# One written list for the chunk loop of a recurrence that feeds a mixture of experts: preparation five chunks ahead, two strided transposes, filler products spread

## The chip, the cores and the metric

The kernel runs on one core of a Trainium2 chip. The core's engines work beside each other and meet through semaphores: TensorE (PE in the profile, its weight loads are PEld) multiplies and transposes into PSUM, VectorE (DVE) and ScalarE (ACT) work on whole tiles, GpSimd (POOL) masks and scatters, and SyncE (SP) issues most of the DMA transfers. Each engine takes its instructions strictly in the order in which they are written for it. The metric is device time in microseconds (us); smaller is better.

## What is computed

The program is a linear recurrence over 768 positions for 4 x 8 heads of width 40, and then a layer of eight experts, of which each row uses the best one. Cut to what matters:

```python
for t in range(S):                                   # attention, S = 768
    y[:, :, t] = einsum('bhd,bhde->bhe', r_t, state)
    Sa = einsum('bhde,bhe->bhd', state, a_t)
    state = state * w_t - outer(Sa, b_t) + outer(v_t, k_t)
...
logits = x @ w_gate                                  # x is y, 3072 rows of 320
expert_idx = argmax(logits)
for e in range(8):
    out[mask_e] = gate_w[mask_e] * (relu(x[mask_e] @ w1[e]) @ w2[e])
```

All data are 32-bit floats.

## The kernel before

**Tiling.** The recurrence is cut into NC = 24 chunks of C = 32 positions. Inside a chunk it is written in closed form with a 32 x 32 triangular matrix per head, which has to be inverted; between chunks only the state is handed on. All 32 heads go together, as 16 pairs or 8 groups.

**The stages of a chunk.** Each is a Python generator whose parts (between its yields) can be placed one by one in the written order. One letter names each:

- p, preparation of a chunk (`step_prep`): a first part with two scans over the decays w (L231, L233) and a small reciprocal, which then issues the DMA loads of the next chunk's w; a second part with two products (`kbmul` L240, `qmul` L245) that scale k, b, r and a, and then further loads. In the start list its pieces have letters of their own: W and a (loads), s (scan), j and q (the two products).
- E (`step_e`): 16 products of a chunk's scaled rows on TensorE (L254), copies into M2c on ScalarE (`m2`, L262), copies into Q (`m1`, L275), and a triangular mask on POOL (`m1_mask`, L280).
- t (`tops`): the inversion for four chunks at once. Its first part transposes M2c into Tt on VectorE (L285), copies to ML on ScalarE and clears parts of Tt on POOL; 14 steps of two VectorE operations each follow (L297, L299); its last part transposes Tt into Tc2 (L302) and Tc (L303).
- B (`merge`): finishes one chunk's inverse: products (L314), copies to Q1, named NB (L318), products (L323), copy into Tc (L325).
- The recurrence itself: R (L347, then ScalarE's copy RS<-psS, L350), U (L357, copies L362), S (L371, then VectorE's product into SVR, L376), and SVR is what the next chunk's R reads.
- The output side: T, K and u are transposes on TensorE with copies on ScalarE, A (L409, VectorE's mask L412) and y (L426, L437) give the chunk's result, and r routes two chunks' rows to their experts and sends them out to the DRAM buffer Xs.
- i writes a seventh of Xs with initial values (648 KB each).

Products on TensorE that go to ps_g share four rotating PSUM blocks of one bank each.

**What sets the order.** Nothing is scheduled by the compiler in this part. A start list (START) is written out by hand: it prepares chunks 0 to 12 and, with an @ ahead of a letter, already places most of the parts of chunks 0 to 3. From chunk I0 = 4 a loop places the parts by a fixed pattern of letters (ORDER, one for even and one for odd chunks), in which a number stands for a share of the inversion of the next four chunks (SPLIT). Preparation runs nine chunks ahead (`s = i + 9` in `step_prep`), E eight ahead. KB and Q have NKB = 9 buffers each, so the load of chunk s + 1's KB has to wait until chunk s - 8 has been transposed; it is therefore the last part of p. The w tile (Wt) and the a tile (AT) have one buffer each. START also holds 72 products of a constant tile scn (L668, 128 x 512, bf16) whose results nobody reads. After the loop a short list (TAIL) ends chunk 23, and the expert stage follows with its own order.

Of the kernel before, what the change touches and what calls it, by code (L numbers as in the profile page):

```python
# [13 lines left out]
U8 = mybir.dt.uint8  # L14
# [5 lines left out]
B, H, S, D = 4, 8, 768, 40  # L20
# [4 lines left out]
E = 8  # L25
# [9 lines left out]

ORDER = (".1 R T A p R T A U U E 2.3 B p E B S E y u u K S B 1 B y K r p",
         ".1 R T A p R T A U U E r 2.3 B p E r B S E y u u K S B 1 B y K r p")
SPLIT = (0, 0.3, 0.5, 0.7, 1)  # L40
TAIL = "R A T U b E S y u K r"

START = ("W0 a0 W1 a1 w22 s0 j0 q0 c5 W2 a2 s1 j1 q1 w9 W3 a3 e0 w3 n0 s2 j2 q2 e1 w3 n1 c7 z0 W4 a4 s3 j3 q3 e2 w3 "
# [8 lines left out]
ENGS = {mybir.EngineType.PE, mybir.EngineType.Activation, mybir.EngineType.DVE, mybir.EngineType.Pool,  # L54
        mybir.EngineType.SP}
AALT = 3
I0 = 4

YW = tuple(int(c == NC - 1) for c in range(NC))
AW = tuple(4 * (c == NC - 1) for c in range(NC))  # L60
# [64 lines left out]
def attention(tc, nc, d, ctx, Xs, okt, sent):  # L125
# [53 lines left out]
    at = lambda ring, c: ring[c % len(ring)]  # L179

    flat = lambda t: t.rearrange("p a b->p (a b)")
    early = lambda s: (0, 1, 2, 0, 2, 0, 2)[s] if s < 7 else 0

    def buf(s):
        v = lambda t: t[:, 0:528].rearrange("p (a b)->p a b", b=33)
# [51 lines left out]
    def kbmul(s, eng):  # L237
        f = buf(s)[1]
        kb = at(KB, s).rearrange("p a (k i)->p a k i", k=2)
        eng.tensor_tensor(kb, kb, f[:, :, 0:32].unsqueeze(2).broadcast_to([128, 16, 2, 32]), ALU.mult)  # L240
        G_.tensor_copy(F0[:, s, :], f[:, :, 32])

    def qmul(s, eng):
        g = gview(s).unsqueeze(2).broadcast_to([128, 16, 2, 32])
        eng.tensor_tensor(at(Q, s), buf(s)[2].rearrange("p t a i->p a t i"), g, ALU.mult)  # L245
# [11 lines left out]
    def m2(s, e):  # L257
        m2, n0 = M2c[0], (s % 4) * 8
        for j in range(2):
            for ty in range(2):  # L260
                bb = 32 * (j * 2 + ty)
                A.copy(m2[bb:bb + 32, :, n0:n0 + 8].rearrange("p t n->p n t"), e[j][32:64, :, ty])  # L262

    def m1v(s, e):
        q = at(Q, s)
# [16 lines left out]

    def tops(k):
        def first():
            V.transpose(flat(Tt), flat(M2c[0]))  # L285
            A.copy(at(ML, k)[:, 0:32], M2c[0][:, 0:16, :].rearrange("p t n->p n t"))
            G_.memset(Tt[:, 0:16, 16:32], 0.0)
            for h in (16, 8, 4, 2, 1):
                G_.memset(bass.AP(Tt.tensor, Tt[:, h, 0:1].offset, [Tt.ap[0], [66 * h, 16 // h], [32, h], [1, h]]), 0.0)
            G_.memset(flat(Tt)[:, 0:1024:33], -1.0)  # L290

        def step(j):
            n = 15 - j
            t = tmp[:, :2 * j * n].rearrange("p (h a b)->p h a b", a=j, b=n)
            bcast = lambda a0, b0, sa, sb: bass.AP(Tt.tensor, Tt[:, a0, b0:b0 + 1].offset,
                                                   [Tt.ap[0], [528, 2], [sa, j], [sb, n]])
            V.tensor_tensor(t, bcast(0, j, 32, 0), bcast(j, j + 1, 0, 1), ALU.mult)  # L297
            u = bcast(0, j + 1, 32, 1)
            V.tensor_tensor(u, u, t, ALU.subtract)  # L299

        def last():
            V.transpose(flat(Tc2), Tt.rearrange("p a b->p b a")[:, 16:32])  # L302
            V.transpose(flat(at(Tc, k)), flat(Tt))  # L303

        return [(2, first)] + [(2 * (0.12 + 2 * j * (15 - j) / 960), lambda j=j: step(j)) for j in range(14, 0, -1)] + [
            (3.1, last)]

    def merge(c):
        t, m, n0 = at(Tc, c // 4), flat(at(ML, c // 4)), c % 4 * 8
        quads = [slice(bb, bb + 32) for bb in range(0, 128, 32)]  # L310
        q = g4([128, 8, 16])
        for x in range(8):
            for b in quads:
                TE.matmul(q[b, x], m[b, (n0 + x) * 16:(n0 + x) * 16 + 32], Tc2[b, :, n0 + x],  # L314
                          start=True, stop=True, tile_position=(b.start, b.start))
        yield
        for b in quads:
            A.copy(Q1[b, :, b.start % 64 + 16:b.start % 64 + 32], q[b])  # L318
        yield
        z = g4([128, 8, 16])  # L320
        for x in range(8):
            for b in (slice(0, 64), slice(64, 128)):
                TE.matmul(z[b, x], Q1[b, x], t[b, 0:16, n0 + x], start=True, stop=True, tile_position=(b.start, b.start))  # L323
        yield
        A.copy(t[:, 0:16, n0:n0 + 8].rearrange("p a n->p n a"), z)  # L325

    def kbt(c):
        kb, ks = at(KB, c), at(KS2, c)
# [23 lines left out]
    def ustage(c):  # L352
        sv, t, rs = at(SVS, c), at(Tc, c // 4), held["rs"]
        u = psU[:, 0:320].rearrange("p (h e)->p h e", e=40)
        for h in range(8):
            for bb in range(0, 128, 32):
                TE.matmul(u[bb:bb + 32, h], t[bb:bb + 32, :, c % 4 * 8 + h], rs[bb:bb + 32, h, bb // 32 % 2 * 40:bb // 32 % 2 * 40 + 40],  # L357
                          start=True, stop=True, tile_position=(bb, bb))
        yield
        for bb in range(4):  # L360
            j, ty = divmod(bb, 2)
            A.copy(sv[32:64, j * 8:j * 8 + 8, TO[ty]:TO[ty] + 40], u[32 * bb:32 * bb + 32])  # L362
# [195 lines left out]
        if i < NC:  # L558
            yield from ustage(i)

    def step_e(i):
        s = i + 8
        if s < NC:
            e = estage(s)
            yield
            m2(s, e)
            yield
            m1(s, e)
            m1_mask(s)
# [20 lines left out]
        if 0 <= i - 1 < NC:  # L590
            yield from route_a(i - 1, held["x"])

    def step_prep(i):
        s = i + 9
        if s < NC:
            scan(s)
            if s + 1 < NC:
                load_w(s + 1, kb=False)
            yield
            kbmul(s, V)  # L600
            qmul(s, V)
            if s + 1 < NC:
                load_a(s + 1)
                yield
                load_kb(s + 1)

    def step_merge(i):
        if i < NC:
# [9 lines left out]
             "S": step_s, "y": step_y, "u": step_ut, "K": step_kbt, "r": step_route, "p": step_prep,  # L618
             "B": step_merge}
    es = {}  # L620
    with tc.manual_schedule(engines=ENGS):
        to = tops(0)
        gens = {}
        for op in START.split():
# [46 lines left out]
            elif op[0] == "c":  # L671
# [18 lines left out]
                if n == 7:  # L690
# [4 lines left out]
    manual = tc.manual_schedule(engines=ENGS)
    manual.__enter__()
    for i in range(I0, NC):
        tl = []
        if 4 * (i // 4 + 1) < NC:
            o, at_ = tops(i // 4 + 1), 0.0  # L700
            tot = sum(w_ for w_, _ in o)
            for w_, f in o:
                if SPLIT[i % 4] - 1e-9 <= at_ / tot < SPLIT[i % 4 + 1] - 1e-9:
                    tl.append((w_, f))
                at_ += w_

        def invert(n):
            while tl and n > 0:
                w_, f = tl.pop(0)
                f()  # L710
                n -= w_

        if True:
            for step in ORDER[i % 2].split():
                if step in steps:
                    k = step + str(i - (step == "r" and i % 2) + (step == "B"))
                    if k not in gens:
                        gens[k] = steps[step](int(k[1:]))
                    next(gens[k], None)
                else:  # L720
                    invert(float(step))
            invert(99)
            for k in list(gens):
                if k != f"r{i}":
                    for _ in gens.pop(k):
                        pass
# [321 lines left out]
```

## Time and profile before

| | |
|---|---|
| time, median of 3 runs | 695.79 us (692.59 to 697.78) |
| the profiled execution | 697.46 us, of which its span 695.7 us |
| mean granted TensorE clock over the span | 0.869 |
| TensorE busy, the recurrence up to 456.7 us | 390.8 us |
| moved by DMA | 93.59 MB, 135 GB/s on average |

The span is the time from the first to the last instruction. [...] In the rows of the profile a line such as L350 is a line of the kernel above, `out<-in` names the tiles without buffer numbers, and idle time stands with the engine and operation that ended it.

### The profile page before, as it was taken

The numbers are of one execution on the slowest core, as the hardware profiler recorded it, in microseconds if no ns is written. First come the engines' busy times: TensorE is split into PE (matmuls) and PEld (weight loads), VectorE is DVE, ScalarE is ACT, GpSimd is POOL, SyncE is SP. The second block draws the span as 40 slices with busy tenths as digits, with TensorE's granted clock in tenths as the row PEclk, the third lists the DMA queues.
The fourth block names the chain that finished last, engine by engine and source line by source line (L and its number), as shares of the span: only waits on it lengthen the run. The fifth ranks groups of instructions, "written<-read, shape, count | busy, mean of one in ns | idle before, by whom it ended". The sixth has DMA issues, their size and how long they took to land.

```text
span 695.7 us, 27306 instructions
## 1 busy us (share of the span) xinstructions
PE 618.5 (89%) x11867; PEld 560.5 (81%) x11867; DVE 446.3 (64%) x876; ACT 399.7 (57%) x915; POOL 125.5 (18%) x239
## 2 busy tenths in 40 slices
PE   7477888579999989799999999989999999999994
PEld 3246778568888879798889888769999999999994
DVE  8895457898768585767554323368567577585641
ACT  2635777677677777778855765455436345255220
POOL 1331212232212121212301101110110211201111
PEclk9676788569787787889996989969999999999997
DMA  7887345524444343443332323488473564552101
GB/s 213 195 219 211 108 130 169 148 88 114 131 113 134 107 127 108 126 112 99 102 100 85 88 92 95 133 257 258 127 233 110 170 224 129 169 185 81 57 0 33
DMA packets 47318, 93.59 MB, mean 135 GB/s; under 512 B 10553, under 2 KB 27066, under 8 KB 47128
## 3 DMA queue, kind: packets, MB, share of 16 engines
q1 hardware_dynamic: 44632, 83.85, 41.1%
q0 software_dynamic: 2560, 7.92, 3.2%
q8 instruction: 96, 1.57, 1.0%
q14 instruction: 30, 0.25, 0.1%
HBM read 79.19 MB, written 13.21 MB: 133 GB/s over the span
## 4 chain that ended last, share of the span: by engine, by line
PE 62%; ACT 12%; issue 10%; DMA 7%; DVE 7%; SPq 1%; POOL 0%; POOLq 0%; DVEq 0%; ACTq 0%
PE ps_g L323 4%; PE psS L347 4%; PE psS L371 4%; PE ps_g L409 4%; PE psY L426 4%; DMA out<-yo,tok 3%; PE m_yp L857 3%; PE m_yp L858 3%; PE m_yp L859 3%; PE m_hp L839 3%; PE m_hp L838 3%; PE ps_g L254 3%; PE m_hp L840 3%; PE ps_g L393 3%; PE psU L357 3%
## 5 line engine op out<-in xcount | busy, mean ns | idle before, releaser
L412 DVE TENSOR_TENSOR Y<-ps_g,mask 64x512 f32<-64x512 f32 x48 | 32.8, 684 | 78.6 <-PE ps_g L409 78.1
L262 ACT COPY M2c<-ps_g 32x256 f32<-32x256 f32 x96 | 57.7, 601 | 31.2 <-PE ps_g L254 29.7
L871 POOL DMA_INDIRECT out<-yo,tok x32 | 30.6, 958 | 200.3 <-DVE yo L870 136.9
L857 PE MATMUL m_yp<-w2h,hx 128*128 128x320 f32 x192 | 60.9, 317 | 0.0
L858 PE MATMUL m_yp<-w2l,hx 128*128 128x320 f32 x192 | 59.2, 308 | 0.0
L859 PE MATMUL m_yp<-w2h,hx 128*128 128x320 f32 x192 | 59.1, 308 | 0.0
L846 DVE SCALAR_TENSOR_TENSOR hx<-m_hp,hx 128x384 fp32r<-128x384 f32 (+1 forms) x128 | 42.7, 386 | 24.3 <-ACT hx L844 24.0
L844 ACT ACTIVATE hx<-m_hp 128x448 fp32r<-128x448 f32 x64 | 34.9, 545 | 40.3 <-PE m_hp L842 40.3
L376 DVE TENSOR_TENSOR SVR<-psS,F 40x640 f32<-40x640 f32 x46 | 37.8, 822 | 29.8 <-PE psS L371 29.2
L371 PE MATMUL psS<-SVS,KS 128*40 128x40 f32 x1472 | 43.1, 220 | 13.1 <-ACT SVS L362 5.7
L280 POOL TENSOR_SCALAR_AFFINE_SELECT Q<-Q 32x512 f32<-32x512 f32 x48 | 37.5, 781 | 90.5 <-ACT Q L275 81.3
L371 PEld LDWEIGHTS psS<-SVS,KS 128*40 128x40 f32 x1472 | 37.4, 133 | 18.8 <-ACT SVS L362 9.3
L362 ACT COPY SVS<-psU 32x320 f32<-32x320 f32 x96 | 40.0, 417 | 18.5 <-PE psU L357 16.7
L338 ACT COPY KS<-ps_g 64x416 f32<-64x416 f32 x96 | 49.0, 510 | 1.2
L254 PE MATMUL ps_g<-Q,KB 128*64 128x64 f32 x768 | 36.5, 267 | 14.1 <-DVE Q L245 7.1
L347 PE MATMUL psS<-SVR,Q 128*64 128x80 f32 x768 | 44.3, 288 | 4.2 <-DMA SVR<-in_VR 4.2
L838 PE MATMUL m_hp<-x,w1h 128*128 128x448 f32 x128 | 47.4, 370 | 0.4 <-ACT x L822 0.4
L839 PE MATMUL m_hp<-x,w1h 128*128 128x448 f32 x128 | 47.6, 372 | 0.0
L254 PEld LDWEIGHTS ps_g<-Q,KB 128*64 128x64 f32 x768 | 33.0, 178 | 17.9 <-DVE Q L245 8.9
L840 PE MATMUL m_hp<-x,w1l 128*128 128x448 f32 x128 | 47.3, 369 | 0.0
L426 PE MATMUL psY<-Y,KS 128*40 128x32 f32 x1504 | 38.9, 212 | 9.1 <-issue 9.1
L347 PEld LDWEIGHTS psS<-SVR,Q 128*64 128x64 f32 x768 | 39.7, 181 | 8.1 <-POOL Q L280 4.5
(165 smaller groups left out, 1491.8 us busy)
## 6 DMA issues: line engine op xcount, KB each, us to landing
w2r<-in_w SPq DMA_DIRECT2D x8, 1280.0 KB
w1r<-in_w SPq DMA_DIRECT2D x8, 1024.0 KB
VU<-in_VT SPq DMA_DIRECT2D x48, 160.0 KB
SVR<-in_VR SPq DMA_DIRECT2D x48, 104.0 KB
SVS<-in_VS SPq DMA_DIRECT2D x24, 208.0 KB
KB<-in_KB SPq DMA_DIRECT2D x30, 160.0 KB
KB<-in_KBP SPq DMA_DIRECT2D x9, 512.0 KB
Xs<-xr SPq DMA_DIRECT2D x7, 648.0 KB
```

Source lines behind the costliest of these rows:

```text
L254: TE.matmul(e[j][:, x], kb[:, p, :], q[:, p], start=True, stop=True, tile_position=(0, 64 * j))
L262: A.copy(m2[bb:bb + 32, :, n0:n0 + 8].rearrange("p t n->p n t"), e[j][32:64, :, ty])
L338: A.copy(ks[0:64, u * 8 + z:u * 8 + 8:2], ts[u][64 * z:64 * z + 64])
L347: TE.matmul(psS[64 * j:64 * j + 64, h, 0:80], q[:, p].rearrange("e t i->e (t i)"), sr[:, :, h, j * 64:j * 64 + 40], start=True, stop=True, ...
L371: TE.matmul(psS[TR[ty], h, j * 40:j * 40 + 40], ks[:, p, o:o + 40], sv[:, p, o:o + 40], start=True, stop=True, tile_position=(0, o))
L426: TE.matmul(py[TR[ty], p], ks[:, p, o:o + 40], y2[:, ty, p, :], start=True, stop=True, tile_position=(0, o))
L838: TE.matmul(hp, w1h[:, k, s], xh[:, k], start=k == 0, stop=False)
L839: TE.matmul(hp, w1h[:, k, s], xl[:, k], start=False, stop=False)
L840: TE.matmul(hp, w1l[:, k, s], xh[:, k], start=False, stop=False)
L857: TE.matmul(yp, hh[:, ft, qs], w2h[:, ft], start=ft == 0, stop=False)
L858: TE.matmul(yp, hh[:, ft, qs], w2l[:, ft], start=False, stop=False)
L859: TE.matmul(yp, hl[:, ft, qs], w2h[:, ft], start=False, stop=ft == 7)
```

## The change

START ends after chunk 3's first E part, the first inversion and R of chunk 0. Everything after it, up to chunk 23, is one list, ORDER, of 751 entries: a letter with its chunk number places the next part of that stage, t the next part of the running inversion, and f two filler products. There are 48 f in it. Preparation now takes the chunk's number from the list, and the list places it five chunks ahead of the recurrence at first (p5 in chunk 0) and up to eight ahead in the middle (p17 in chunk 9); the KB load is issued together with the w load. M2c and Tc are stored with the head index outside, so that the copies and products which touch one head read or write rows without gaps, while the transposes L285 and L303 (L299 and L317 after) read or write with a step. Chunk 1's first Q copies carry the mask with them on VectorE (`m1v`, which was there but unused, L283). Stage A of chunks 0 to 2 uses the form of the later chunks (AALT).

The filler goes to one of the four ps_g blocks; START's went to psY.

```diff
-ORDER = (".1 R T A p R T A U U E 2.3 B p E B S E y u u K S B 1 B y K r p",
+ORDER = ("y0 M2 j4 B0 K0 B0 q4 A0 i0 B0 B0 B1 p5 B1 p5 K0 f U0 E5 p6 U0 S0 S0 E4 u0 p6 i1 E5 E5 f B1 E4 p7 u0 B1 p7 R1  "
...
-AALT = 3
-I0 = 4
+AALT = 0
...
-                A.copy(m2[bb:bb + 32, :, n0:n0 + 8].rearrange("p t n->p n t"), e[j][32:64, :, ty])
+                A.copy(m2[bb:bb + 32, n0:n0 + 8, :], e[j][32:64, :, ty])
...
-            V.transpose(flat(Tt), flat(M2c[0]))
-            A.copy(at(ML, k)[:, 0:32], M2c[0][:, 0:16, :].rearrange("p t n->p n t"))
+            V.transpose(flat(Tt), M2c[0].rearrange("p n t->p t n"))
+            A.copy(at(ML, k)[:, 0:32], M2c[0][:, :, 0:16])
...
-            V.transpose(flat(at(Tc, k)), flat(Tt))
+            V.transpose(at(Tc, k).rearrange("p n a->p a n"), flat(Tt))
...
-    def step_prep(i):
-        s = i + 9
+    def step_prep(s):
         if s < NC:
             scan(s)
             if s + 1 < NC:
-                load_w(s + 1, kb=False)
+                load_w(s + 1)
             yield
             kbmul(s, V)
             qmul(s, V)
             if s + 1 < NC:
                 load_a(s + 1)
-                yield
-                load_kb(s + 1)
...
+        if op == "f":
+            hot = g4([128, 512])
+            for _ in range(2):
+                TE.matmul(hot, scn[:, 0:128], scn[:, 0:512], start=True, stop=True)
+            continue
```

How the order moves is seen at three places. The first is VectorE around the first inversion. KB_87 and Q_88 are chunk 4's tiles, Q_82 is chunk 1's. Before:

```order
L233 SCALAR_TENSOR_TENSOR G_93<-Q_78,RC 128x528
L285 STREAM_TRANSPOSE Tt<-M2c 128x1024
L240 TENSOR_TENSOR KB_87<-KB_87,KB_77 128x1024
L245 TENSOR_TENSOR Q_88<-VU,G_93 128x1024
L297 TENSOR_TENSOR tmp<-Tt 128x28
L299 TENSOR_TENSOR Tt<-Tt,tmp 128x2x14
```

Now, with the end of the inversion:

```order
L247 SCALAR_TENSOR_TENSOR G_93<-Q_78,RC 128x528
L299 STREAM_TRANSPOSE Tt<-M2c 128x1024
L283 TENSOR_TENSOR Q_82<-ps_g,mask 32x8x32 x4
L311 TENSOR_TENSOR tmp<-Tt 128x28
...
L316 STREAM_TRANSPOSE Tc_121<-Tt 128x512
L317 STREAM_TRANSPOSE Tc_115<-Tt 128x32x32
L254 TENSOR_TENSOR KB_87<-KB_87,KB_77 128x1024
L259 TENSOR_TENSOR Q_88<-VU,G_93 128x1024
```

Chunk 4's two products stand behind the inversion, and chunk 1's four masked copies have come to VectorE. The second place is the SP queue's loads after the start, around the w load of chunk 6 (KB_73). Before:

```order
L202 DMA Q_78<-in_W 40x529 x2
L195 DMA KB_73<-in_KBP 128x1024
L208 DMA VU<-in_A 40x16x32
L209 DMA VU<-in_A 40x16x32
L213 DMA SVR<-in_VR 32x832 x2
L214 DMA SVS<-in_VS 32x1664
L680 DMA VU<-in_czero 24x1024 x2
L681 DMA Y_105<-in_czero 24x1024
```

Now:

```order
L239 DMA Y_105<-in_RT 40x512
L240 DMA Y_105<-in_RT 40x512
L231 DMA VU<-in_VT 40x1024
L232 DMA VU<-in_VT 40x1024
L623 DMA Xs<-xr 128x4x324
L216 DMA Wt<-in_W 40x529 x2
L209 DMA KB_73<-in_KBP 128x1024
L222 DMA AT<-in_A 40x512
L223 DMA AT<-in_A 40x512
```

Chunk 6 is loaded behind the first blocks of the loop and one block of Xs, and no longer ahead of chunk 1's values. The third place is TensorE in the middle of the loop, from chunk 10's key transpose (KB_81) past its R (Q_82) to the next recurrence product. Before, where L254 is stage E of chunk 18:

```order
L334 MATMUL ps_g<-ident,KB_81 128x104 x8
L323 MATMUL ps_g<-Tc_115,NB 64x16 x16
L499 MATMUL ps_g<-gt,cg 128x16
L500 MATMUL ps_g<-gt,cg 128x16
L347 MATMUL psS<-SVR,Q_82 64x80 x16
L383 MATMUL ps_g<-ident,SVR 104x40 x16
L409 MATMUL ps_g<-RT,VU 64x2x32 x16
L357 MATMUL psU<-RS,Tc_115 32x40 x32
L254 MATMUL ps_g<-Q_80,KB_79 64x64 x16
```

Now, where L268 is stage E of chunk 17 and L718 the filler:

```order
L348 MATMUL ps_g<-ident,KB_81 128x104 x8
L440 MATMUL psY<-Y_105,KS_123 40x32 x32
L423 MATMUL ps_g<-RT,VU 64x2x32 x16
L268 MATMUL ps_g<-Q_78,KB_77 64x64 x16
L328 MATMUL ps_g<-Tc_121,ML_117 32x16 x32
L361 MATMUL psS<-SVR,Q_82 64x80 x16
L397 MATMUL ps_g<-ident,SVR 104x40 x16
L371 MATMUL psU<-RS,Tc_115 32x40 x32
L440 MATMUL psY<-Y_105,KS_123 40x32 x32
L718 LDWEIGHTS scn
L718 MATMUL ps_g<-scn 128x512
```

Only one transpose now stands between R and U, E stands ahead of R, and a filler pair (the last two rows and two like them) follows y, where the list waits for U's copies; the order differs from chunk to chunk.

More of the change, by code (lines that the diff above doesn't have):

```diff
@@ L33 @@
 TO = (64, 0)
-ORDER = (".1 R T A p R T A U U E 2.3 B p E B S E y u u K S B 1 B y K r p",
-         ".1 R T A p R T A U U E r 2.3 B p E r B S E y u u K S B 1 B y K r p")
-SPLIT = (0, 0.3, 0.5, 0.7, 1)
-TAIL = "R A T U b E S y u K r"
-START = ("W0 a0 W1 a1 w22 s0 j0 q0 c5 W2 a2 s1 j1 q1 w9 W3 a3 e0 w3 n0 s2 j2 q2 e1 w3 n1 c7 z0 W4 a4 s3 j3 q3 e2 w3 "
[8 rows of a table removed]
+ORDER = ("y0 M2 j4 B0 K0 B0 q4 A0 i0 B0 B0 B1 p5 B1 p5 K0 f U0 E5 p6 U0 S0 S0 E4 u0 p6 i1 E5 E5 f B1 E4 p7 u0 B1 p7 R1  "
[23 rows of a table added]
+TAIL = "R A T U b E S y u K r"
+START = ("W0 a0 W1 a1 w22 s0 j0 q0 c5 W2 a2 s1 j1 q1 w9 W3 a3 e0 w3 n0 s2 j2 q2 e1 w3 n1 m0 M0 c7 z0 W4 a4 s3 j3 q3  "
+         "e2 w3 n2 c1 W5 a5 e3 w3 n3 s4 t1 c2 d1 m2 m3 K0 t2 @R0 w3 t2 @R0 c6 w8 t2 w8 t3 w8 t3 c3 w4 t3 w4 ")
 ENGS = {mybir.EngineType.PE, mybir.EngineType.Activation, mybir.EngineType.DVE, mybir.EngineType.Pool,
         mybir.EngineType.SP}
-AALT = 3
-I0 = 4
+AALT = 0
 YW = tuple(int(c == NC - 1) for c in range(NC))
@@ L181, in attention @@
     flat = lambda t: t.rearrange("p a b->p (a b)")
-    early = lambda s: (0, 1, 2, 0, 2, 0, 2)[s] if s < 7 else 0
+    early = lambda s: (0, 1, 2, 0, 2)[s] if s < 5 else 0
     def buf(s):
@@ L322, in merge @@
             for b in (slice(0, 64), slice(64, 128)):
-                TE.matmul(z[b, x], Q1[b, x], t[b, 0:16, n0 + x], start=True, stop=True, tile_position=(b.start, b.start))
+                TE.matmul(z[b, x], Q1[b, x], t[b, n0 + x, 0:16], start=True, stop=True, tile_position=(b.start, b.start))
         yield
-        A.copy(t[:, 0:16, n0:n0 + 8].rearrange("p a n->p n a"), z)
+        A.copy(t[:, n0:n0 + 8, 0:16], z)
     def kbt(c):
@@ L356, in ustage @@
             for bb in range(0, 128, 32):
-                TE.matmul(u[bb:bb + 32, h], t[bb:bb + 32, :, c % 4 * 8 + h], rs[bb:bb + 32, h, bb // 32 % 2 * 40:bb // 32 % 2 * 40 + 40],
+                TE.matmul(u[bb:bb + 32, h], t[bb:bb + 32, c % 4 * 8 + h, :], rs[bb:bb + 32, h, bb // 32 % 2 * 40:bb // 32 % 2 * 40 + 40],
                           start=True, stop=True, tile_position=(bb, bb))
@@ L559, in step_u, with step_e @@
             yield from ustage(i)
-    def step_e(i):
-        s = i + 8
+    def step_e(s):
         if s < NC:
@@ L620, in attention @@
     es = {}
-    with tc.manual_schedule(engines=ENGS):
+    manual = tc.manual_schedule(engines=ENGS)
+    manual.__enter__()
+    if True:
         to = tops(0)
@@ L694, in attention @@
                     DMA.dma_start(Q1, d["cq"])
[L695 to L726, printed above, removed]
+    once = {"j": lambda s: kbmul(s, V), "q": lambda s: qmul(s, V), "M": m1_mask}
+    groups, to, gens = iter(range(1, NC // 4)), [], {}
+    for op in ORDER.split():
+        if op == "t":
+            if not to:
+                to = tops(next(groups))
+            to.pop(0)[1]()
+            continue
[3 more added lines that the diff above has]
+                TE.matmul(hot, scn[:, 0:128], scn[:, 0:512], start=True, stop=True)
+            continue
+        if op[0] in once:
+            once[op[0]](int(op[1:]))
+            continue
+        if op not in gens:
+            gens[op] = steps[op[0]](int(op[1:]))
+        next(gens[op], None)
+    gens = {}
     manual.__exit__(None, None, None)
```

31 rows, old and new, of tables (ORDER, START) are left out of this document.

## The prediction

> **What bounds the kernel now.** I read the page's first part, then busy time by stage, then the times of one instruction that every chunk has once, then single steps, and last the wait lists. The page:
>
> ```profile
> span 695.7 us, 27306 instructions
> PE 618.5 (89%) x11867; PEld 560.5 (81%) x11867; DVE 446.3 (64%) x876; ACT 399.7 (57%) x915; POOL 125.5 (18%) x239
> PE 62%; ACT 12%; issue 10%; DMA 7%; DVE 7%; SPq 1%; POOL 0%; POOLq 0%; DVEq 0%; ACTq 0%
> ```
>
> TensorE carries the chain of waits, but the share is an average. ScalarE's copy RS<-psS (L350) occurs once a chunk and lies on the recurrence, so its starts are the chunk clock (rows of ScalarE's timeline, chunks 0, 5, 14 and 23):
>
> ```profile
> 41.16 0.69 ACT L350 COPY RS<-psS 128x640 f32<-128x640 f32 x1 [2.58 <-PE psS L347]
> ...
> 161.68 0.70 ACT L350 COPY RS<-psS 128x640 f32<-128x640 f32 x1
> ...
> 312.60 0.69 ACT L350 COPY RS<-psS 128x640 f32<-128x640 f32 x1
> ...
> 438.21 0.69 ACT L350 COPY RS<-psS 128x640 f32<-128x640 f32 x1 [0.57 <-ACT lt L453]
> ```
>
> Cut at these times, busy time by stage:
>
> ```profile
> core 0: us, PE busy (x) PEld busy (x) DVE busy (x) ACT busy (x) POOL busy (x), PEclk, DMA share, GB/s
> 0.00:41.20 41.20, 22.48 (x212) 12.97 (x213) 35.76 (x46) 19.72 (x39) 14.12 (x30) 0.77 0.78 202
> 41.20:161.70 120.50, 95.88 (x2323) 84.37 (x2322) 87.75 (x141) 77.16 (x178) 27.62 (x51) 0.75 0.53 152
> 161.70:312.60 150.90, 138.08 (x3951) 127.72 (x3950) 107.52 (x215) 113.72 (x275) 29.80 (x73) 0.81 0.41 117
> 312.60:438.20 125.60, 118.04 (x3719) 108.24 (x3718) 58.01 (x135) 84.13 (x213) 17.81 (x45) 0.91 0.31 93
> 438.20:456.70 18.50, 16.33 (x346) 14.45 (x346) 8.67 (x33) 7.99 (x23) 3.80 (x8) 0.87 0.68 217
> 456.70:695.70 239.00, 227.69 (x1326) 212.74 (x1326) 148.55 (x310) 96.97 (x191) 32.37 (x34) 0.96 0.45 141
> ```
>
> So five steps cost 120.5 us (24.1 each), the next nine 150.9 (16.8 each) and the last nine 125.6 (14.0 each). In the first five no engine is near full: TensorE works 80% and VectorE 73% of the time. From 161.7 on TensorE is busy 92 to 94%, but at a mean granted clock of 0.81 and 0.91: nearly 40% and a fifth of those stretches lie at the lower of its two levels, where the same product takes longer. Single steps at or near the full clock show what a step costs there:
>
> ```profile
> 312.60:326.40 13.80, 12.47 (x445) 11.49 (x443) 11.67 (x20) 11.87 (x28) 4.07 (x6) 1.00 0.39 117
> 326.40:341.10 14.70, 14.25 (x467) 13.19 (x466) 6.65 (x17) 13.66 (x34) 3.01 (x7) 1.00 0.26 78
> 341.10:353.30 12.20, 11.01 (x390) 9.76 (x385) 5.84 (x15) 8.07 (x22) 2.22 (x9) 1.00 0.39 120
> 383.30:396.70 13.40, 12.20 (x407) 11.41 (x406) 5.51 (x16) 8.72 (x26) 0.89 (x5) 1.00 0.30 86
> 411.00:424.20 13.20, 12.80 (x421) 11.97 (x421) 5.41 (x16) 8.68 (x24) 0.87 (x5) 0.98 0.29 86
> ```
>
> The first two still hold a preparation product (stage E), the other three don't: 14.25 us with it, 12.9 without. Why the early part is slow, from the list of waits and the DMA issues:
>
> ```profile
> ACT M2c L262 <- PE ps_g L254: 29.7, 6, 12.4
> PE ps_g L254 <- DMA KB<-in_KB: 5.5, 1, 5.5
> 41.20:67.80 26.60, 22.10 (x449) 16.87 (x449) 20.41 (x34) 11.25 (x28) 0.74 (x3) 0.76 0.82 219
> KB<-in_KB SPq DMA_DIRECT2D x30, 160.0 KB
> KB<-in_KBP SPq DMA_DIRECT2D x9, 512.0 KB
> Xs<-xr SPq DMA_DIRECT2D x7, 648.0 KB
> ```
>
> At the seam between the start list and the loop TensorE waits 5.5 us for a KB slot, and ScalarE up to 12.4 us behind it. The first step moves 219 GB/s.
>
> **The change, part by part.** The work stays; it is dealt out anew. From the new list I count what stands between the copies of chunks 0 and 5: nine scan parts, nine multiply parts, five S, five A, four y, one route part, 14 inversion steps, two first and one last transpose part. The rows:
>
> ```profile
> L231 DVE TENSOR_TENSOR_SCAN FF<-Wt,scn 128x528 f32<-128x528 f32 x20 | 24.8, 1239 | 3.3 <-POOL F L241 1.8 <-DMA Wt<-in_W 1.4
> L245 DVE TENSOR_TENSOR Q<-AT,G 128x1024 f32<-128x1024 f32 x20 | 24.5, 1227 | 0.0
> L376 DVE TENSOR_TENSOR SVR<-psS,F 40x640 f32<-40x640 f32 x46 | 37.8, 822 | 29.8 <-PE psS L371 29.2
> L412 DVE TENSOR_TENSOR Y<-ps_g,mask 64x512 f32<-64x512 f32 x48 | 32.8, 684 | 78.6 <-PE ps_g L409 78.1
> L285 DVE STREAM_TRANSPOSE Tt<-M2c 128x1024 f32<-128x1024 f32 x6 | 7.4, 1233 | 1.8 <-ACT M2c L262 1.8
> L302 DVE STREAM_TRANSPOSE Tc<-Tt 128x512 f32<-128x512 f32 x6 | 6.4, 1067 | 0.1
> L262 ACT COPY M2c<-ps_g 32x256 f32<-32x256 f32 x96 | 57.7, 601 | 31.2 <-PE ps_g L254 29.7 <-ACT SVS L362 0.2
> L275 ACT COPY Q<-ps_g 32x256 f32<-32x256 f32 x96 | 34.8, 362 | 1.6
> ```
>
> A scan part is two scans and a small reciprocal, 2.75 us; a multiply part two products of the L245 kind, 2.45; S 2 x 0.82; A 2 x 0.68; an inversion step about 0.56; y and route about 0.7 and 0.9. That is 24.8 + 22.0 + 8.2 + 6.8 + 2.7 + 0.9 + 7.8 = 73.2, and 7.5 for the transposes (below): 80.7 us of VectorE. DMA in the same steps: three KBP and five KB pairs, the W and A of eight chunks, seven Xs blocks, the streams of five chunks (some 1.06 MB each) and 2 MB left over from the start, 17.6 MB; at 219 GB/s an estimate of 80 us. So neither allows less than 81. The list mixes both evenly, and with preparation five to eight ahead the KB slot asked for is free by then, so the 5.5 us wait and its train go. The nearest row for what VectorE can hold is step 312.6 to 326.4, 11.67 of 13.80 (85%), and the seam step at its best 90%; 80.7 at 88% gives 92 us. Gain 28.5; bounds 84 and 98.
>
> **Transposes and copies.** M2c is now written in rows: the copies of L262, scattered at 601 ns, should cost what L275 does for the same shape, 362: 0.96 us less ScalarE per chunk. In exchange L285 reads and L303 writes with a 128-byte step. L302 already reads so: 1067 ns for 512 elements, 2.08 ns each against 1.2 in L285. I take that rate for both, 2.13 us instead of 1.23; between nothing and 0.9 us each, two per four chunks. Counted above in the first steps; later VectorE is busy only 71% and covers it. [...]
>
> **Filler products.** 48 pairs of 512-column products, 13 in the first five steps, 34 in the next 18. Their price, from the warm-up products already there:
>
> ```profile
> 445.00 1.02 PE L416 MATMUL psY<-scn 128*128 128x512 bf16 x4
> 22.01 1.22 PE L668 MATMUL psY<-scn 128*128 128x512 bf16 x3
> ```
>
> 0.26 us each at the full clock and 0.41 at the half: 0.5 us a pair, so 17 us in the 18 steps if nothing hides them, and nothing if all fall into TensorE's idle time, which those 276.5 us hold 20.4 of. What they may give back is the clock. Before it fell at 364 us TensorE had run 2.14 of 3 us:
>
> ```profile
> 360.00:363.00 3.00, 2.14 (x43) 1.94 (x37) 2.07 (x6) 0.59 (x1) 0.11 (x2) 1.00 0.44 125
> 363.00:366.00 3.00, 3.00 (x46) 2.86 (x46) 0.40 (x3) 1.39 (x4) 0.00 (x0) 0.60 0.29 80
> 366.00:369.00 3.00, 3.00 (x46) 2.75 (x42) 0.54 (x3) 1.81 (x4) 1.02 (x1) 0.50 0.15 55
> ```
>
> 46 products in 3 us there, against about 100 in full-clock stretches. For the 18 steps: the new list holds 12 E products there, so at the full clock 12 x 14.25 + 6 x 12.9 = 249 us (13.8 a step). Half of the fillers on the path adds 8.5. Of the clock I take a twentieth of the time at the lower level, between none and the fifth of the last nine steps and nearer none, since the pairs stand behind products that wait: 14 us, in which by the two rows above a product takes 1.6 times as long, so 5 us lost. Together 262 us, 14.55 a step, against 276.5. Gain 14.5; bounds 249 and 279 (all fillers paid and the clock of the last nine steps, 15.5 a step).
>
> **Parts with one answer.** The first inversion runs with one pair of POOL masks beside it instead of four, and chunk 4's two products move behind it; four mask products of chunk 1 come to VectorE (about 0.4 us each) while it would wait for POOL to clear Tt. Chunk 0's U may start a few us sooner; since VectorE and the DMA queue bound the next step, I count nothing. On the SP queue KB now stands ahead of A: 512 KB are 2.4 us at 219 GB/s, less than the scan part of 2.75 us that comes before A is read; nothing, and up to 2.4 us in each of the three early preparations if that cover is gone, which the bound of 98 holds. The Xs writes move on the same queue from three at once to single ones between loads, the same bytes. Stage A of chunks 0 to 2 puts both halves of its products into one block, as later chunks do: one pass instead of two, under 1 us of TensorE a chunk, which waits there anyway; nothing. The tail and the expert stage (18.5 and 239 us) keep their code and order: nothing.
>
> Sum against the profiled execution's 697.46: 697.5 - 28.5 - 14.5 = 654.5. It stands 1.7 above the median of 695.8, so the predicted median is 653.
>
> **Rivals.** One: the clock holds and the fillers hide. 84 + 249 us gives 697.5 - 36.5 - 27.5 - 1.7, about 632. For it speaks that idle time and fillers are of one size; against it, that fillers sit at fixed places and idle time does not. Two: the fillers are plain extra work and the clock stays as it is late in the loop. 98 + 279 gives 697.5 - 22.5 + 2.5 - 1.7, about 676. For it: TensorE is busy 94% there as it is. Three, the change does nothing: the dealt-out order costs in the 18 steps (17 us, 16.3 a step) what the early steps win, 689 to 700. Against it: no late step of this work was that slow at a high clock. Four, slower: a filler takes one of the four rotating ps_g blocks, so TensorE must wait until ScalarE has read that block's previous content, with the recurrence queued behind it. A full group of four L275 copies is 1.45 us; 48 of them cost 70 us and the time is 723. It decides from 43 / 48 = 0.9 us a filler. Against it: the copies that free blocks run all the time, and TensorE's waits on ScalarE are now short.
>
> **How the numbers follow.** My case (640 to 668) 0.48, rival one 0.18, rival two 0.19, no change 0.07, slower 0.08. A difference under 1% (7 us) can't be told from none here. Faster is 0.48 + 0.18 + 0.19 = 0.85, same 0.07, slower 0.08. The range from 629 to 681 leaves out the last two cases and a little of the first two rivals.
>
> **What would show it.** Right: copies of chunk 5 near 133 us and of chunk 23 near 395, no step over 25 us, M2c copies near 0.36 us, transposes near 2.1, a mean granted clock above 0.9 from chunk 5 on. Wrong: TensorE waits on ScalarE ahead of fillers or of the products behind them; a clock near 0.8 still; VectorE under 80% and the DMA queue under 180 GB/s in the first five steps, which would mean that the new order waits on itself; transposes well over 2.1 us.

## The result and the profile after

The changed kernel is faster: 670.99 us in the median of four runs (665.97 to 676.89) against 694.19 us (689.13 to 697.78) on the same chip, a ratio of 0.9647 with a 95% interval of 0.955 to 0.9744. The gain is 23 us; 43 were forecast (28.5 and 14.5), and the time lies inside the range. The profiled execution is the slowest of the four, 676.89 us, some 6 above the median, and its span is 20.5 us shorter than the one before. Ratios, here and below, leave out disturbed runs, which the medians and ranges hold, so that a ratio is not the quotient of two medians.

Line numbers of the chunk stages grew by 14 (L350 is L364 now, L262 is L276). "After" and "before" stand for the changed kernel and the one before. The head of the page and its chain of waits, after:

```profile
span 675.2 us, 27495 instructions
PE 618.3 (92%) x11969; PEld 540.4 (80%) x11969; DVE 452.4 (67%) x881; ACT 374.0 (55%) x911; POOL 141.7 (21%) x236
PE 73%; ACT 5%; DMA 5%; issue 4%; DVE 4%; SPq 1%; POOL 0%; DVEq 0%; ACTq 0%
```

TensorE's busy time is what it was, in a shorter span. The chunk clock, from ScalarE's timeline, at chunks 0, 5, 14 and 23:

```profile
40.42 0.69 ACT L364 COPY RS<-psS 128x640 f32<-128x640 f32 x1 [4.88 <-PE psS L361]
...
132.26 0.69 ACT L364 COPY RS<-psS 128x640 f32<-128x640 f32 x1
...
282.97 0.69 ACT L364 COPY RS<-psS 128x640 f32<-128x640 f32 x1 [0.51 <-PE psS L361]
...
418.42 0.69 ACT L364 COPY RS<-psS 128x640 f32<-128x640 f32 x1 [1.65 <-PE psS L361]
```

Cut there, the busy time by stage (columns as before: stretch, length, busy time and count of PE, PEld, DVE, ACT and POOL, granted clock, DMA share, GB/s):

```profile
0.00:40.40 40.40, 23.40 (x212) 13.61 (x213) 35.63 (x59) 14.08 (x34) 12.18 (x26) 0.79 0.79 204
40.40:132.30 91.90, 82.04 (x2398) 65.15 (x2399) 77.96 (x111) 65.22 (x173) 25.57 (x43) 0.96 0.65 193
132.30:283.00 150.70, 142.36 (x3930) 124.24 (x3928) 107.69 (x218) 101.96 (x268) 39.21 (x74) 0.82 0.38 114
283.00:418.40 135.40, 128.11 (x3806) 112.32 (x3805) 75.91 (x162) 88.70 (x230) 29.49 (x60) 0.90 0.32 95
418.40:436.50 18.10, 14.59 (x305) 12.40 (x305) 6.40 (x24) 6.49 (x17) 2.42 (x3) 0.90 0.73 229
436.50:675.20 238.70, 227.82 (x1327) 212.65 (x1326) 148.80 (x311) 97.56 (x192) 32.80 (x34) 0.96 0.45 140
```

The granted clock stands at two levels in both profiles: of the half-microsecond slices of after 1083 of 1340 have 1.00, 230 have 0.50 and 27 a number between, none less; of those of before it is 1010, 333 and 37 of 1380. So a row's clock c is read here as a mean of the two, with 2(1 - c) of the row at the lower one. There the same work takes longer: U's 64 products of a chunk took 0.79 us at 1.00 and 1.29 at 0.50 (101.42 and 204.37 us in after).

So the first five steps fell from 120.5 to 91.9 us, and their clock rose from 0.75 to 0.96. The 18 steps after them, 276.5 us before, take 286.1 (150.7 + 135.4). The clock there is no better: 0.82 and 0.90 against 0.81 and 0.91. Start, tail and expert stage together are within 2 us of before. In this execution all of the gain is in five steps, and the later loop gave a third of it back.

The same kernel was profiled a second time with the experiments, in an execution of 667.61 us, nearer its median. Its five early steps and its 18 later ones:

```profile
41.70:132.50 90.80, 80.90 (x2383) 66.83 (x2397) 78.07 (x105) 65.10 (x172) 26.66 (x42) 0.93 0.65 194
132.50:408.60 276.10, 253.49 (x7712) 225.04 (x7732) 183.39 (x379) 190.59 (x497) 68.44 (x134) 0.91 0.37 108
```

The early gain is the same. The later steps take 276.1 us at a clock of 0.91, against 276.5 at 0.85 before: here they give nothing back, but they gain nothing either, although the clock is higher.

Of the first two profiles, the 18 later steps in one row each, before and after:

```profile
161.70:438.20 276.50, 256.12 (x7666) 235.96 (x7665) 165.54 (x349) 197.85 (x488) 47.62 (x117) 0.85 0.36 106
```

```profile
132.30:418.40 286.10, 270.47 (x7733) 236.56 (x7731) 183.59 (x379) 190.66 (x497) 68.70 (x133) 0.86 0.36 105
```

TensorE is idle for 15.6 us in place of 20.4, but busy for 14.4 us more. The groups that the change touches, over the whole span of after (count, busy us, mean ns, idle before):

```profile
L276 ACT COPY M2c<-ps_g 32x256 f32<-32x256 f32 x96 | 35.0, 364 | 27.7 <-PE ps_g L268 26.3 <-ACT KS L352 0.2
L718 PE MATMUL ps_g<-scn 128*128 128x512 bf16 x96 | 31.9, 433 | 0.9 <-ACT Q L289 0.9
L371 PE MATMUL psU<-RS,Tc 32*32 32x40 f32 x1536 | 21.7, 207 | 5.4 <-ACT RS L364 2.9 <-issue 2.4
L371 PEld LDWEIGHTS psU<-RS,Tc 32*32 32x32 f32 x1536 | 18.0, 113 | 11.5 <-issue 4.7 <-ACT RS L364 4.2 <-ACT NB L332 1.7
L299 DVE STREAM_TRANSPOSE Tt<-M2c 128x1024 f32<-128x1024 f32 x6 | 11.7, 1956 | 3.6 <-ACT M2c L276 3.5
L317 DVE STREAM_TRANSPOSE Tc<-Tt 128x1024 f32<-128x1024 f32 x6 | 11.5, 1916 | 0.0
```

and U's two rows before, which the prediction did not show:

```profile
L357 PE MATMUL psU<-RS,Tc 32*32 32x40 f32 x1536 | 28.7, 237 | 0.9 <-ACT RS L350 0.9
L357 PEld LDWEIGHTS psU<-RS,Tc 32*32 32x32 f32 x1536 | 25.5, 150 | 3.4 <-ACT RS L350 1.1 <-ACT Tc L325 0.5
```

The 96 fillers are 31.9 us of TensorE and waited 0.9 us in all (2.3 us for ScalarE in the second profile). U's weight loads, which now read rows without gaps, fell from 150 to 113 ns and its products from 28.7 to 21.7 us: a gain on the bounding engine that the prediction did not list.

### The profile page after: what moved, and what is told of

The parts are those of the page before. It is cut to its first block, busy times and chain, and to the rows that moved or that the text cites. A ratio compares the mean times of both kernels' runs of the same rounds, so it can differ in the third digit from the quotient of the medians.

```text
span 675.2 us, 27495 instructions
## 1 busy us (share of the span) xinstructions
PE 618.3 (92%) x11969; PEld 540.4 (80%) x11969; DVE 452.4 (67%) x881; ACT 374.0 (55%) x911; POOL 141.7 (21%) x236
## 4 chain that ended last, share of the span: by engine, by line
PE 73%; ACT 5%; DMA 5%; issue 4%; DVE 4%; SPq 1%; POOL 0%; DVEq 0%; ACTq 0%
PE psY L440 5%; PE m_yp L857 4%; PE m_yp L858 4%; PE m_yp L859 4%; PE psS L385 4%; PE psS L361 4%; PE m_hp L839 4%; PE m_hp L838 4%; PE m_hp L840 4%; PE ps_g L423 4%; PE ps_g L337 3%; PE ps_g L718 3%; PE ps_g L407 3%; PE ps_g L348 2%; DMA Y<-in_RT 2%
## 5 line engine op out<-in xcount | busy, mean ns | idle before, releaser
L294 POOL TENSOR_SCALAR_AFFINE_SELECT Q<-Q 32x512 f32<-32x512 f32 x46 | 51.1, 1111 | 56.1 <-ACT Q L289 50.7
L276 ACT COPY M2c<-ps_g 32x256 f32<-32x256 f32 x96 | 35.0, 364 | 27.7 <-PE ps_g L268 26.3
L523 POOL DMA_INDIRECT Xs<-xr,si x24 | 25.4, 1057 | 116.8 <-DMA Xs<-xr,si 24.9
L361 PE MATMUL psS<-SVR,Q 128*64 128x80 f32 x768 | 38.9, 266 | 7.4 <-DMA SVR<-in_VR 5.4
L401 ACT COPY KS<-ps_g 40x320 f32<-40x320 f32 x92 | 38.6, 419 | 8.7 <-PE ps_g L397 6.8
L361 PEld LDWEIGHTS psS<-SVR,Q 128*64 128x64 f32 x768 | 34.9, 162 | 9.1 <-issue 5.9
L268 PE MATMUL ps_g<-Q,KB 128*64 128x64 f32 x768 | 30.9, 235 | 10.3 <-DVE Q L259 5.3
L440 PEld LDWEIGHTS psY<-Y,KS 128*40 128x40 f32 x1504 | 34.6, 130 | 6.5 <-issue 4.2
```

The source lines that it names most:

```text
L294: G_.affine_select(q[o:o + 32, :, ty], q[o:o + 32, :, ty], pattern=[[0, 16], [-1, 32]], base=0, channel_multiplier=1, compare_op=ALU.is_gt ...
L361: TE.matmul(psS[64 * j:64 * j + 64, h, 0:80], q[:, p].rearrange("e t i->e (t i)"), sr[:, :, h, j * 64:j * 64 + 40], start=True, stop=True, ...
L440: TE.matmul(py[TR[ty], p], ks[:, p, o:o + 40], y2[:, ty, p, :], start=True, stop=True, tile_position=(0, o))
```

## The experiments

Ten further kernels ran, and after and the kernel without fillers ran a second time. The theories in the expectations: P, the fillers are work that is paid for on the path; W, rival four, a filler costs by the ps_g block that it waits for; L, the written list is no better than the old pattern once the early steps are past; C, M, Y and Z are told in the expectations. Medians, and each kernel's ratio to the kernel before on its own chip:

| kernel | median us (range, runs) | ratio [95%] |
|---|---|---|
| after | 670.99 (665.97–676.89, 4) | 0.9647 [0.955, 0.9744] |
| no fillers | 663.21 (653.59–678.87, 6) | 0.9524 [0.9431, 0.9617] |
| fillers into psU | 673.25 (664.47–682.65, 6) | 0.9705 [0.9613, 0.9797] |
| old layout | 677.66 (673.43–700.09, 7) | 0.9807 [0.9728, 0.9886] |
| early list, pattern with catch-up | 683.05 (673.04–691.83, 6) | 0.9832 [0.9726, 0.9937] |
| before with the new layout | 689.8 (680.22–697.41, 12) | 0.9922 [0.987, 0.9974] |
| early fillers only | 676.63 (664.14–683.15, 6) | 0.9659 [0.9555, 0.9763] |
| early list, pattern eight ahead | 668.66 (664.32–678.03, 6) | 0.9634 [0.9562, 0.9705] |
| half of each filler | 666.69 (655.05–670.22, 6) | 0.9514 [0.9419, 0.961] |
| a quarter of each filler | 665.59 (654.58–670.84, 6) | none |
| late half only | 661.79 (652.74–670.8, 6) | 0.9515 [0.9442, 0.9588] |
| after again | 666.36 (659.99–678.04, 6) | 0.9599 [0.9535, 0.9662] |
| no fillers again | 665.84 (650.31–669.96, 6) | 0.9455 [0.9376, 0.9534] |

**How runs were compared at one clock.** Runs of one kernel differ by 10 to 27 us, and they follow their granted clock. A span s at mean clock c spent 2(1 - c)s at the lower level. Over 121 runs of all kernels, each against its own kernel's mean, a microsecond at the lower level goes with 0.34 us of time (correlation 0.90; one run of before, at a clock of 0.692 and 755 us, is left out). Taking 0.35 of that time off the mean time gives what the kernel would take at the full clock, an estimate (with 0.34 every row is 1 to 2 us higher). The fit does not show which way the cause runs: a run that waits more could also be granted a lower clock.

| kernel (runs) | mean clock | us at the lower level | mean us | at the full clock |
|---|---|---|---|---|
| before (38) | 0.877 | 171 | 695.0 | 635 |
| after, both times (10) | 0.920 | 107 | 668.4 | 631 |
| no fillers, both times (12) | 0.899 | 134 | 663.2 | 616 |
| half / quarter of each (6, 6) | 0.915 / 0.908 | 113 / 122 | 665.0 / 665.0 | 625 / 622 |
| late half only (6) | 0.913 | 114 | 660.5 | 620.5 |
| early fillers only (6) | 0.888 | 151 | 675.6 | 623 |
| fillers into psU (6) | 0.925 | 100 | 674.4 | 639 |
| old layout (7) | 0.915 | 116 | 685.0 | 644 |
| early list, catch-up / eight ahead (6, 6) | 0.891 / 0.898 | 149 / 136 | 682.7 / 670.6 | 630.5 / 623 |
| before with the new layout (12) | 0.879 | 167 | 688.8 | 630 |

The last column of each of the two kernels that ran twice came out within 2 us (632 and 630; 616.5 and 616), and that of before on the three chips where it ran beside them, too (635, 635 and 636.5). Its standard errors are 0.4 to 1.9 us.

**No fillers**

```diff
         if op == "f":
-            hot = g4([128, 512])
-            for _ in range(2):
-                TE.matmul(hot, scn[:, 0:128], scn[:, 0:512], start=True, stop=True)
             continue
```

> The changed kernel without the 48 filler pairs of the list (the start's fillers stay). Theory P, the fillers are plain work on a full TensorE and do not hold the clock: the time falls by most of the 23 us that they are busy for after chunk 5, to 650 to 662 us, and the clock of the 18 steps stays at 0.82 to 0.90. Theory C, they hold the clock: the clock of the 18 steps falls below 0.80 and the time is 671 to 690.

> The kernel without fillers in the list once more, beside the changed one: 658 to 668 us, about 134 us at the lower clock and a rest near 616.

> The changed kernel once more, beside the ones without fillers on the same chip: 668 to 674 us, 8 us or more above e12 if theory P holds.

Only the list's fillers are left out; the start list's stay. Without them the clock falls from 0.920 to 0.899, and the time does not rise. The two stages in the profile without them:

```profile
38.00:132.10 94.10, 84.05 (x2359) 72.58 (x2360) 80.51 (x117) 65.36 (x173) 25.73 (x45) 0.84 0.63 189
132.10:412.30 280.20, 259.69 (x7676) 238.95 (x7676) 181.30 (x378) 190.20 (x498) 67.73 (x129) 0.83 0.36 107
```

The later steps' clock of 0.83 lies where P had it, and the time a little above P's range. The early gain stands without fillers at a clock of 0.84 (94.1 us in place of 91.9; 96.9 at 0.83 when it ran again), so the new order made most of it, not the fillers. At the full clock the fillers cost 631 - 616 = 15 us, about half of their 31.9 us of TensorE; they save 28 us at the lower level, 9.5 us. The net is some 5 us lost (668.4 against 663.2, standard errors 1.9 and 2.4). On the chip where both ran again the medians agree within a microsecond while the ratios differ by 0.0144; so what is shown is that the fillers bring no gain, not that they cost one; the 8 us between the two that P asked for there did not come.

**Smaller doses, and where they stand**

```diff
-            for _ in range(2):
+            for _ in range(1):
```

> One product per filler in place of two, all 48 places. If the cost is the products themselves and the hold on the clock goes with their number, half way between the kernel without fillers and the changed one: 665 to 669. If the place alone holds the clock, the clock stays near 0.917 and the time is 660 to 664.

```diff
-            hot = g4([128, 512])
-            for _ in range(2):
-                TE.matmul(hot, scn[:, 0:128], scn[:, 0:512], start=True, stop=True)
+            hot = g4([128, 512])[:, 0:256]
+            TE.matmul(hot, scn[:, 0:128], scn[:, 0:256], start=True, stop=True)
```

> One product of 256 columns per filler, a quarter of the changed kernel's columns in the same 48 places. The relation of all runs so far is time = rest + 0.34 x (time at the lower clock). If the place holds the clock, some 113 us at the lower clock as with two products and with one, a rest near 620: 656 to 661 us. If the columns hold it, about 125 us there: 661 to 666.

```diff
-            for _ in range(2):
+            if "R5" in gens:
+                hot = g4([128, 512])
                 TE.matmul(hot, scn[:, 0:128], scn[:, 0:512], start=True, stop=True)
```

> One product per filler, and only behind chunk 5's R (35 places). Early fillers alone (e6) came out at 676 against 663 without any. If early fillers do harm, 652 to 660; if e6 lay high by the spread of the runs, 663 to 668, as with all 48.

```diff
+            if "R5" in gens:
+                continue
             hot = g4([128, 512])
```

> The changed kernel with the 13 filler pairs up to chunk 5's R and without the 35 behind it. Theory P (fillers behind chunk 5 cost more than they return, the early ones hide under VectorE and DMA): 655 to 664 us, first five steps at a clock above 0.9. If late fillers earn their cost: 668 or more.

Half of the products holds the clock nearly as high (0.915, 0.913 against 0.920), and at the full clock the doses line up with their number: 616 with none, 620.5 with 35, 625 with 48, 631 with 96, some 0.13 to 0.19 us a product; 48 products of half the columns give 622. That is P's side of it. "Late half only" has the lowest median of all kernels, 661.8 us, but it can't be told from no fillers, from half or from a quarter: their medians lie within 5 us, and the runs of each spread over more than 15. The early ones alone came out badly against P, under which leaving out the late ones had to gain: 676.6 us, at a clock below that of no fillers (0.888 against 0.899). At the full clock they stand at 623, or 0.27 us for each of 26 products, above the others; that, and why the clock stood lower in those six runs, is open.

**Fillers into a block of their own**

```diff
-            hot = g4([128, 512])
-            for _ in range(2):
-                TE.matmul(hot, scn[:, 0:128], scn[:, 0:512], start=True, stop=True)
+            for w in (192,) * 5 + (64,):
+                TE.matmul(psU[:, 320:320 + w], scn[:, 0:128], scn[:, 0:w], start=True, stop=True)
```

> The same columns of filler (1024 a pair), written to the unused columns of psU in pieces of 192 and 64, so that no filler takes a ps_g block. Theory W, the cost of a filler is its wait for one of four rotating blocks, and that of the product which finds one block fewer: 655 to 665 us, with no wait of TensorE on ScalarE ahead of a filler. Theory P or C: 668 to 675, as the changed kernel (six weight loads a pair in place of two may add a few us).

No ps_g block is taken, and the time is no shorter (673.25 us). But it is not a clean swap. The pieces lie in psU, the tile of U's results:

```profile
L717 PE MATMUL psU<-scn 128*128 128x192 bf16 x240 | 30.0, 266 | 5.2 <-ACT SVS L376 5.2
L717 PE MATMUL psU<-scn 128*128 128x64 bf16 x48 | 9.8, 204 | 0.0
```

The same columns now take 39.8 us of TensorE in place of 31.9, and wait 5.2 us for ScalarE's copies of U. This version is 8 us slower than after at the full clock, so it can't decide on W. The waits in the traces do. All waits of TensorE for ScalarE and VectorE ahead of products into ps_g, fillers and others together, are 10.6 and 13.2 us in the two profiles with fillers and 14.8 and 15.2 in the two without. The fillers don't lengthen them, and W is out.

**The layout, taken back and put in alone**

The first kernel is after with before's layout of M2c and Tc (seven lines), the second is before with the new one. The core of the second:

```diff
-                A.copy(m2[bb:bb + 32, :, n0:n0 + 8].rearrange("p t n->p n t"), e[j][32:64, :, ty])
+                A.copy(m2[bb:bb + 32, n0:n0 + 8, :], e[j][32:64, :, ty])
...
-            V.transpose(flat(Tt), flat(M2c[0]))
+            V.transpose(flat(Tt), M2c[0].rearrange("p n t->p t n"))
...
-            V.transpose(flat(at(Tc, k)), flat(Tt))
+            V.transpose(at(Tc, k).rearrange("p n a->p a n"), flat(Tt))
...
-                TE.matmul(u[bb:bb + 32, h], t[bb:bb + 32, :, c % 4 * 8 + h], rs[bb:bb + 32, h, bb // 32 % 2 * 40:bb // 32 % 2 * 40 + 40],
+                TE.matmul(u[bb:bb + 32, h], t[bb:bb + 32, c % 4 * 8 + h, :], rs[bb:bb + 32, h, bb // 32 % 2 * 40:bb // 32 % 2 * 40 + 40],
```

> The changed kernel with M2c and Tc laid out as before, so transposes read and write without steps and the copies scatter. Forecast from the prediction's rows: VectorE gains 0.9 us in each of 12 transposes, ScalarE pays 0.24 us in each of 96 copies; both have room late in the loop, so 671 to 677. If a layout is what slows the 18 steps, 660 or less; if the early steps lean on it, 680 or more.

> The kernel before with only the new layout of M2c and Tc. Theory Y, the layout pays by itself since TensorE's weight loads of U read rows without gaps (U's products 7 us less busy in the changed kernel) and ScalarE has 28 us less to do: 676 to 684 us, at a clock as before. Theory Z, the layout only pays under the new order: 688 to 694.

Taken back it costs 7 us in the medians and 13 at the full clock; put in alone it gains 5.5 us (0.9922, interval below one), though its time lies where Z had it. Groups of after with the old layout:

```profile
L276 ACT COPY M2c<-ps_g 32x256 f32<-32x256 f32 x96 | 57.4, 598 | 25.1 <-PE ps_g L268 23.6 <-ACT KS L352 0.4
L371 PE MATMUL psU<-RS,Tc 32*32 32x40 f32 x1536 | 28.9, 229 | 8.6 <-ACT RS L364 4.3 <-issue 3.9
L371 PEld LDWEIGHTS psU<-RS,Tc 32*32 32x32 f32 x1536 | 25.3, 147 | 14.9 <-issue 7.2 <-ACT RS L364 5.6 <-ACT NB L332 1.3
```

and of before with the new one:

```profile
L357 PE MATMUL psU<-RS,Tc 32*32 32x40 f32 x1536 | 22.1, 215 | 0.0
L357 PEld LDWEIGHTS psU<-RS,Tc 32*32 32x32 f32 x1536 | 18.9, 120 | 2.2 <-ACT Tc L325 0.4
L285 DVE STREAM_TRANSPOSE Tt<-M2c 128x1024 f32<-128x1024 f32 x6 | 11.7, 1942 | 0.0
```

In either order of work the layout takes 22 us from ScalarE's M2c copies and about 7 from TensorE's U, and adds about 9 to VectorE's two transposes. How much of the time comes from U and how much from the copies was not separated. Most of the early gain is the order's. The five steps in the new order with the old layout, and in the old order with the new layout:

```profile
40.80:135.10 94.30, 85.64 (x2400) 70.13 (x2399) 78.04 (x111) 73.96 (x172) 26.56 (x46) 0.93 0.62 187
38.80:149.10 110.30, 87.29 (x2310) 76.75 (x2309) 89.86 (x141) 67.66 (x178) 27.52 (x51) 0.81 0.57 165
```

**The list after the early steps**

Both kernels follow the new list up to chunk 5's R, with its fillers, and then the old pattern without any. The first keeps the old distance of nine chunks, so that step 5 has to place two preparations and two E in place of one each; the second places p eight and E seven ahead, and nothing is left to catch up. Of the second:

```diff
-    for op in ORDER.split():
+    words = ORDER.split()
+    for op in words[:words.index("R5")]:
...
+        for step in (FIVE if i == 5 else PATTERN[i % 2]).split():
+            if step[0] in steps:
+                s = step[0]
+                k = step if len(step) > 1 else s + str(
+                    i - (s == "r" and i % 2) + (s == "B") + 7 * (s == "E") + 8 * (s == "p"))
```

> The new list up to chunk 5's R, then the loop and pattern of before (nine ahead, one chunk's backlog caught up in step 5, no fillers after chunk 4). Theory L, the list wins only in the first five steps and its late part is no better than the pattern: 18 steps near 276 us, total 655 to 668. Theory M, the mixed late order is better than the pattern and something else hides it: 672 or more.

> As e4, but without a step that catches up: after chunk 5's R the old pattern with preparation eight and E seven ahead, so no 30 us step; early fillers kept. Theory L, the late list is no better than the old pattern: within 6 us of e6, and step 5 to 6 at 18 us or less. Theory M, the late list is worth something: 8 us or more above e6.

Step 5, and the 17 steps behind it, of the second kernel:

```profile
130.40:150.90 20.50, 13.90 (x352) 13.12 (x351) 15.24 (x41) 11.61 (x33) 4.60 (x11) 0.75 0.26 81
150.90:409.90 259.00, 237.14 (x7272) 218.19 (x7271) 165.09 (x326) 176.18 (x464) 48.19 (x114) 0.86 0.37 109
```

and step 5 of the first:

```profile
131.80:161.80 30.00, 16.55 (x377) 15.27 (x377) 21.80 (x47) 14.60 (x40) 7.87 (x14) 0.73 0.27 80
```

The catch-up brings the seam back: a step of 30 us, against 30.5 in before, with TensorE busy for little more than half of it, and the kernel loses more than half of the gain (683 us; its time alone, without this step, would have spoken for M). Without catch-up the old pattern takes 668.7 us. That is less than the written list with the same early fillers (676.6), and equal to it at the full clock (623 each). That is 8 us below the early fillers only, where L had within 6 and M had 8 above, and step 5 takes 20.5 us, not the 18 of L. M is out: no worth of 18 steps of hand-placed order over the pattern shows. The list up to chunk 5, and the smaller distance behind it, are what counts.

## Why the prediction came out at half the gain

- **First term, the early steps: right, with some luck.** 91.9 us against 92 (90.8 in the second profile). The seam step is gone, the KB wait is no longer among TensorE's largest waits there, DMA moved 193 GB/s, and no step is over 25 us (the longest is 24.6, chunk 0 to 1). VectorE holds 77.96 of 91.9 us: the work is less than the 80.7 forecast and the share, 85%, less than the 88% taken, and the two misses cancel. The 12.4 us of ScalarE that the prediction put behind the KB wait lie elsewhere: that wait ended at 14.47 us, in the start list (`14.47 0.60 ACT L262 COPY M2c<-ps_g 32x256 f32<-32x256 f32 x1 [12.36 <-PE ps_g L254]`); behind the KB wait ScalarE waited 5.6 us.
- **Second term, the 18 later steps: wrong.** 262 us forecast; 286.1 and 276.1 measured, the first beyond its bound of 279. The step that failed is the clock: "Of the clock I take a twentieth of the time at the lower level, between none and the fifth of the last nine steps and nearer none, since the pairs stand behind products that wait". The two profiles have 0.86 and 0.91, so 28% and 18%, or 80 and 50 us at the lower level; at 0.35 that is 28 and 17 us, not 5.
- **The parts of that term**, as estimates. Fillers on the path: 15 us for 96 products is 11 for the 68 there, against 8.5. The price of one at the lower level, 0.41 us, was read from a row whose mean clock was 0.62; four in after took 0.47 each at 0.50, which would have put the clock's loss at 6 us in place of 5. What is left is 286 - 28 - 11 = 247 us, and 276 - 17 - 11 = 248, against the forecast base of 249. But the row of before, 276.5 us at 0.85, is 83 us at the lower level, and 276.5 - 29 gives 247 too. So the base was right and was no gain: all that the second term had to win was the clock, which rose from 0.85 to 0.86 or 0.91, and the fillers' own work ate what it gave. Rival two, "the fillers are plain extra work and the clock stays as it is late in the loop", put 279 on these steps. The two profiles lie on either side of that: its mechanism is the one that held, and only its 98 for the early steps was too high.
- **Of what the whole gain is made**, by the table at one clock, again as an estimate. From before to after 27 us are gained in the means, of which 22 go with the clock (64 us less at the lower level) and 4 remain at the full clock. Without fillers 19 remain and 13 go with the clock. Most of the clock's part lies in the five early steps, whose time at the lower level fell from 60 us (0.75 of 120.5) to 7 or 13: the first term, worked out from VectorE and DMA alone, came out by its number and did not reckon with this. How much of the early gain the clock made is not separated; without fillers, at 0.84 and 0.83, 24 to 26 of the 28.6 us are there.
- **Copies and transposes: sizes right, the list too short.** M2c copies 364 ns (362 forecast), transposes 1.96 and 1.92 us (2.13 forecast). Beyond the early steps the layout stood at nothing; it is worth 5 to 13 us, and U's weight loads were not seen as touched. So the total holds a gain that the forecast lacked.
- **Rival four, the wait for a block: out.** 0.9 and 2.3 us in all against the 43 from which it decides. Start, tail and expert stage at nothing: right within 2 us.

Why the fillers held the clock so little is seen at one place where it fell. TensorE's timeline in after:

```profile
180.50 0.60 PE L718 MATMUL ps_g<-scn 128*128 128x512 bf16 x2
181.03 0.63 PE L371 MATMUL psU<-RS,Tc 32*32 32x40 f32 x46
182.24 0.40 PE L371 MATMUL psU<-RS,Tc 32*32 32x40 f32 x18 [0.57 <-issue]
183.58 1.86 PE L718 MATMUL ps_g<-scn 128*128 128x512 bf16 x4 [0.95 <-ACT Q L289]
```

and its busy time and clock there:

```profile
180.00:183.00 3.00, 2.06 (x130) 1.45 (x121) 2.96 (x4) 2.89 (x8) 2.81 (x4) 1.00 0.21 60
183.00:186.00 3.00, 2.42 (x16) 1.02 (x17) 3.00 (x3) 2.82 (x10) 2.94 (x3) 0.59 0.83 230
186.00:207.00 21.00, 21.00 (x430) 18.72 (x430) 10.47 (x29) 9.47 (x23) 3.47 (x11) 0.50 0.28 91
207.00:210.00 3.00, 3.00 (x86) 2.81 (x85) 1.73 (x4) 2.58 (x9) 0.00 (x0) 0.93 0.50 160
```

A pair ran at 180.5, TensorE then stood idle between U's products, and the next pair came late, because it too waited, 0.95 us for ScalarE. In this place a filler, in TensorE's written order, ran before or after the idle stretch and not in it. The clock fell when the four products came (1.00 from 183.0 to 183.5 us, 0.55 in the next half microsecond, then 0.50; they took 0.47 us each, against 0.30 for the pair before), and they did not raise it. In the second profile the step at this place is as long, 23.5 us: its copies RS<-psS start at 180.67 and 204.15 us, here at 179.8 and 203.3. That the idle stretch made the clock fall is argued from the order of events, not shown; after other such stretches it did not fall:

```profile
96.00:99.00 3.00, 1.60 (x54) 1.46 (x52) 2.82 (x8) 2.88 (x9) 1.42 (x2) 1.00 0.65 205
99.00:108.00 9.00, 7.77 (x237) 6.39 (x236) 8.51 (x22) 6.51 (x19) 2.82 (x8) 1.00 0.82 260
```

## What to carry to other kernels

Where a loop runs slow at its start, cut the profile at an instruction that occurs once a step, and smooth the seam between prologue and loop before touching the steady part: here five steps of 23 held all of the gain. Price filler products as work on the path, about half of it here (15 of 31.9 us), and count on the clock they should hold only after a run has shown it; half of the dose held it nearly as high (0.915 against 0.920). When a layout changes, list every reader and writer of the tile with its engine: here the forecast left out U's weight loads and products, on the engine that bounds the loop.

## What the runs showed of the hardware

- A microsecond at the lower level of the clock went with 0.34 us of time, over 121 runs (correlation 0.90).
- Between 186 and 207 us in after TensorE was busy for all of 21 us at the lower level, two fillers among the products, and the granted clock stayed at 0.50; at 207 to 210 it rose (0.93 in that row). What raised the clock these runs don't show.
- A weight load of 32 x 32 fp32 that reads with a 128-byte step takes 147 to 150 ns, without gaps 113 to 120, with either order of the work: 150 in before and 120 with the new layout put in, 113 in after and 147 with the old layout put back.
